# A replanned start: batch 0 partly on GpSimd, a shared interface in the planner, and longer fillers on TensorE

## The chip, the cores and the metric

The kernel runs on one core of one Trainium2 chip. The metric is the device time of an execution in microseconds (us), taken over several runs. A core has five engines that run their own instruction queues: TensorE (PE, matrix products; PEld is its weight load), VectorE (DVE), ScalarE (ACT), GpSimd (POOL) and SyncE (SP, which issues the DMAs here). They wait for each other only through semaphores.

## The reference, cut to what matters

Attention over 4 batches, 8 heads, 576 positions of width 64, in two parts that are added: attention over means of 4 positions (144 x 144 scores per head), and local attention over a band of 3 positions to either side. Its output, 2304 tokens of width 512, goes through a two-layer network with a softplus between.

```python
q_d = q.reshape(B, H, Sd, factor, D).mean(axis=3)      # k_d, v_d alike
out_up = np.repeat(sm_attn(q_d, k_d, v_d), factor, axis=2)
mask = np.abs(pos[:, None] - pos[None, :]) < factor
scores = np.where(mask, scale * np.matmul(q, k.transpose(0, 1, 3, 2)), -1000000000.0)
...
attn = attn / (np.sum(attn, axis=-1, keepdims=True) + 1e-09)
x = (out_up + np.matmul(attn, v)) as [2304, 512]
h = x @ w_in                                            # 512 x 2048
g = np.maximum(h, 0.0) + np.log1p(np.exp(-np.abs(h)))
out = g @ w_out                                         # 2048 x 512
```

## The kernel before, in words

**The work.** Attention is done in 16 units (a batch and a pair of heads; units 0 to 3 are batch 0, `u < NPAIR`, called early). The network works on 5 groups of 512 tokens (the last has 256): layer 1 makes for each of 16 blocks `f` of the inner width a bank `h`, layer 2 adds its product into four banks `acc`. Each operand is split into a high and a low part (`xh`/`xl`, `wi..h`/`wi..l`, `gh`/`gl`), and three products are taken of each pair, so a step of layer 1 or 2 is 12 products of 512 columns.

**One unit of attention.** q and k arrive by DMA. Their sums over 4 positions are made (on TensorE in batch 0, as products with the identity into the bank `sums`, line 331; by a reduction on DVE later, line 344, tiles `qd` and `kd`). ACT scales `qd` into `block`. TensorE makes the scores of the means (`psd`, line 379) and of the band (`psc`, lines 432 and 439). DVE takes maxima (`mxd`, `mx`), ACT the exponentials, DVE sums and reciprocals, and the weights are divided (`sd`: on ACT in batch 0; `sc`: on POOL). They are transposed (`pdt` on TensorE, copied by ACT to `sdT`; `sT` on DVE). The sums of v over 4 positions are `vd` (line 360 on DVE in batch 0, lines 365 and 368 on POOL in batch 1 and on DVE later). TensorE makes `po` (lines 530 and 538), DVE adds both parts into `x` (line 558), ACT and DVE split it into `xh` and `xl` (lines 573 and 578).

**Weights.** A block of `w_in` or `w_out` arrives in 64 bits an element, in one of four buffers that rotate under the tag `stage`. ACT makes a narrow copy `top` (line 631), DVE joins it with the rest (line 636), ACT casts the high part (line 655), and DVE, or POOL for `w_in` from block 4 on, subtracts the low part (line 661). A buffer is free for the DMA of the fourth block after it when that is done.

**Between the layers.** Of a bank `h`, ACT makes the softplus in three passes (lines 702, 705, 706), DVE the last step `t` (line 711), POOL the high part `gh` (line 720), and POOL (first group) or DVE (other groups) the low part `gl` (line 728).

**What sets the order.** All of it is recorded as operations with an engine, a cost, a priority and what they read and write. `Plan.order` runs through a planned time and picks for each free engine the ready operation of lowest priority; the engines then execute their lists in that order. `Plan.warm` puts filler products (`busy`, line 829, a product of 384 columns that nobody reads) into the gaps that TensorE has in the plan ahead of layer 1.

## Time and profile before

| what | us |
|---|---|
| median of 3 runs (516.05 to 516.4) | 516.07 |
| the profiled execution | 515.83 |
| its span, first to last instruction | 513.8 |
| PE busy in it | 499.9 |
| DVE busy | 273.4 |
| ACT busy | 249.8 |
| POOL busy | 121.3 |

The profiled execution's time is 2.03 us above its span. The profile lists for each instruction when it ran, and for an engine that stood idle what ended the wait. Products are pipelined and their ends are modelled, so one of them reads longer (0.39 us) than its distance to the next (0.23 us).

### The profile page before, as it was taken

Reading aid. Unit: us, or ns where it says so; the run is one execution under the profiler, and the core shown is the slowest. Engines: PE = TensorE matmul, PEld = TensorE weight load, DVE = VectorE, ACT = ScalarE, POOL = GpSimd, SP = SyncE. Lnnn points to the kernel's source line nnn. Section 1 sums busy time; section 2 is a strip of 40 time slices with the busy share of each in tenths; the row PEclk is TensorE's granted clock in tenths of the full one; section 3 lists DMA queues with packets and bytes.
Section 4 is the critical chain, followed back from the end, with each engine's and each line's share of the span. In section 5 each row is a group of like instructions: output and inputs, shape, how many; then the busy total and the mean of one; then the engine's idle time right before and its main releaser. Section 6 shows DMA issues by size and latency. Waiting matters only on the chain.

```text
span 513.8 us, 12554 instructions
## 1 busy us (share of the span) xinstructions
PE 499.9 (97%) x5407; PEld 414.2 (81%) x5407; DVE 273.4 (53%) x476; ACT 249.8 (49%) x543; POOL 121.3 (24%) x149
## 2 busy tenths in 40 slices
PE   7999889999899999999999999999999999999997
PEld 6877668888678888887888888888888888889996
DVE  4669976989886564545364746352332222223222
ACT  2468887775765444444354334343343233234442
POOL 2101548775751120102010201120100100101110
PEclk9999999999999999999999999999999999999999
DMA  8914744764622311111112212100020000002001
GB/s 269 340 38 130 245 141 151 245 237 154 200 71 80 136 48 57 48 53 50 55 48 90 96 34 70 33 3 1 0 83 0 1 0 0 1 1 83 1 1 41
DMA packets 15798, 42.86 MB, mean 83 GB/s; under 512 B 1792, under 2 KB 2304, under 8 KB 15744
## 3 DMA queue, kind: packets, MB, share of 16 engines
q1 hardware_dynamic: 15744, 42.07, 25.0%
q8 instruction: 42, 0.69, 0.6%
q14 instruction: 12, 0.10, 0.1%
HBM read 37.35 MB, written 4.72 MB: 82 GB/s over the span
## 4 chain that ended last, share of the span: by engine, by line
PE 80%; DVE 10%; ACT 4%; POOL 3%; issue 2%; POOLq 0%; DVEq 0%
PE acc L747 33%; PE h L682 32%; PE po L538 4%; PE sums L331 3%; DVE wro L636 3%; PE psc L439 2%; PE psd L379 2%; PE po L530 2%; PE pdt L508 1%; DVE wri L636 1%; ACT top L631 1%; PE busy L829 1%; POOL gl L728 1%; DVE t L711 1%; ACT t L705 1%
## 5 line engine op out<-in xcount | busy, mean ns | idle before, releaser
L711 DVE SCALAR_TENSOR_TENSOR t<-h,t 128x512 f32<-128x512 f32 (+1 forms) x80 | 50.8, 636 | 142.4 <-ACT t L706 142.4
L720 POOL TENSOR_SCALAR gh<-t 128x512 fp32r<-128x512 f32 (+1 forms) x80 | 52.2, 653 | 302.8 <-PE acc L747 153.1
L702 ACT ACTIVATE t<-h 128x512 f32<-128x512 f32 (+1 forms) x80 | 44.4, 555 | 153.5 <-PE h L682 134.1
L682 PE MATMUL h<-xh,wi0h 128*128 128x512 f32 (+1 forms) x160 | 61.2, 382 | 1.2 <-ACT wi0h L655 1.2
L747 PE MATMUL acc<-gh,wo0h 128*128 128x512 f32 (+1 forms) x160 | 60.2, 376 | 0.8 <-POOL gh L720 0.8
L728 DVE TENSOR_TENSOR gl<-t,gh 128x512 fp32r<-128x512 f32 (+1 forms) x64 | 39.9, 623 | 39.2 <-POOL gh L720 39.2
L747 PE MATMUL acc<-gl,wo0h 128*128 128x512 f32 (+1 forms) x160 | 59.2, 370 | 1.2 <-POOL gl L728 1.2
L682 PE MATMUL h<-xh,wi0l 128*128 128x512 f32 (+1 forms) x160 | 59.6, 373 | 0.6 <-POOL wi0l L661 0.6
L682 PE MATMUL h<-xh,wi1h 128*128 128x512 f32 (+1 forms) x160 | 60.2, 376 | 0.0
L747 PE MATMUL acc<-gh,wo1h 128*128 128x512 f32 (+1 forms) x160 | 59.6, 372 | 0.0
L682 PE MATMUL h<-xl,wi0h 128*128 128x512 f32 (+1 forms) x160 | 59.6, 372 | 0.0
L682 PE MATMUL h<-xh,wi1l 128*128 128x512 f32 (+1 forms) x160 | 59.5, 372 | 0.0
L682 PE MATMUL h<-xl,wi1h 128*128 128x512 f32 (+1 forms) x160 | 59.4, 371 | 0.0
L747 PE MATMUL acc<-gh,wo0l 128*128 128x512 f32 (+1 forms) x160 | 59.3, 370 | 0.0
L747 PE MATMUL acc<-gl,wo1h 128*128 128x512 f32 (+1 forms) x160 | 59.1, 369 | 0.0
L747 PE MATMUL acc<-gh,wo1l 128*128 128x512 f32 (+1 forms) x160 | 59.0, 369 | 0.0
L706 ACT ACTIVATE t<-t 128x512 f32<-128x512 f32 (+1 forms) x80 | 47.3, 591 | 2.5
L705 ACT ACTIVATE t<-t 128x512 f32<-128x512 f32 (+1 forms) x80 | 47.2, 590 | 2.4
L682 PEld LDWEIGHTS h<-xh,wi0l 128*128 128x128 f32 x160 | 30.2, 189 | 6.9 <-POOL wi0l L661 1.1
L682 PEld LDWEIGHTS h<-xh,wi0h 128*128 128x128 f32 x160 | 30.0, 188 | 7.0 <-ACT wi0h L655 1.6
L747 PEld LDWEIGHTS acc<-gl,wo0h 128*128 128x128 f32 x160 | 30.1, 188 | 6.5 <-POOL gl L728 1.5
L747 PEld LDWEIGHTS acc<-gh,wo0h 128*128 128x128 f32 x160 | 30.0, 188 | 6.2 <-POOL gh L720 1.0
(93 smaller groups left out, 827.0 us busy)
## 6 DMA issues: line engine op xcount, KB each, us to landing
wri<-in_w_in_dram SPq DMA_DIRECT2D x16, 511.8 KB, 4.5
wro<-in_w_out_dram SPq DMA_DIRECT2D x16, 511.8 KB, 4.7
vw<-in_vwin_dram SPq DMA_DIRECT2D x16, 384.0 KB, 4.2
qT<-in_qt_dram SPq DMA_DIRECT2D x16, 292.0 KB, 3.0
kT<-in_kt_dram SPq DMA_DIRECT2D x16, 292.0 KB, 5.7
stage<-in_vrow_dram SPq DMA_DIRECT2D x16, 288.0 KB
out_dram<-osb SPq DMA_DIRECT2D x16, 256.0 KB, 2.2
out_dram<-osb SPq DMA_DIRECT2D x4, 128.0 KB, 1.8
```

The lines of the kernel that those rows point to most:

```text
L331: nc.tensor.matmul(sums.t[:, i * SD : (i + 1) * SD], ident, v[:, :, f], start=(f == 0), stop=(f == FACTOR - 1),)
L379: nc.tensor.matmul(pd3()[:, r, :], qb[:, r * RD : (r + 1) * RD], kd.t, start=True, stop=True)
L538: nc.tensor.matmul(po[h].t[j * D : (j + 1) * D, t * HT : (t + 1) * HT], vw.t[kp, t, :], sT.t[kp, t, :HT], start=True, stop=True,)
L636: lambda: nc.vector.scalar_tensor_tensor(out=e(), in0=e(), scalar=13, in1=top.rearrange("p e w -> p (e w)").bitcast(I32), op0=ALU.logical_ ...
L682: nc.tensor.matmul(h.t[:, :n], w[:, cc, fs], x.t[:, cc, :n], start=(cc == 0 and k == 0), stop=(cc == NCC - 1 and k == 2),)
L702: op("ACT", c, pr, lambda: nc.scalar.activation(out=tv(), in_=hh(), func=AF.Abs), r=[h], w=[tt])
L705: nc.scalar.activation(out=tv(), in_=tv(), func=AF.Exp, scale=-1.0)
L706: nc.scalar.activation(out=tv(), in_=tv(), func=AF.Ln, bias=1.0)
L711: lambda: nc.vector.scalar_tensor_tensor(out=tv(), in0=hh(), scalar=0.0, in1=tv(), op0=ALU.max, op1=ALU.add),
L720: lambda: nc.gpsimd.tensor_scalar(out=gh.t[:, :n], in0=tv(), scalar1=1.0, scalar2=0.0, op0=ALU.mult, op1=ALU.add),
L728: lambda: eng[ge].tensor_tensor(out=gl.t[:, :n], in0=tv(), in1=gh.t[:, :n].bitcast(F32), op=ALU.subtract),
L747: nc.tensor.matmul(acc[g][m].t[:, :n], w[:, f % FB, ms], a.t[:, :n], start=(f == 0 and k == 0), stop=(f == NF - 1 and k == 2),)
```

## The change

Every operation that uses the interface to SBUF which DVE and POOL share is marked `port`, and the planner never lets two of them run at once. In batch 0 the sums of q and k go from TensorE to DVE (the reduction of the later batches), the sums of v, the division of `sd` and the low part `xl` go from DVE and ACT to POOL. In the first group of the network the low parts `gl` go from POOL to DVE, as do those of `w_in` from block 4 on, and the sums of v of batch 1. The small constant ahead of the reciprocals is no longer added by a `tensor_scalar`: it stands in the second column of a prepared pair, and a reduction over the pair adds it. Costs of the planner are changed, block 3 of group 0 no longer takes an `acc` bank, the priority of the `w_out` blocks is one later, and each gap of TensorE ahead of layer 1 that holds at least two fillers gets two more.

```diff
+V_POOL = (0,)
+NORM0 = "POOL"
+O_POS = 4
+NSPLIT = 3
+BLOCK0 = "ACT"
+XL_POOL = (0,)
...
-    FILL = 0.2
+    FILL = 0.165
...
-    DMA_RATE = 0.24
+    DMA_RATE = 0.33
...
+        o.kb, o.block, o.port = kb, block, port or eng == "POOL"
...
+                    if o.port and port > t + 1e-9:
+                        continue
...
+                if o.port:
+                    port = o.end
...
                 n = int((o.start - last) / self.FILL)
+                if n > 1:
+                    n += 2
...
-        if early:
+        if u in ON_PE:
             sums = bank("acc", f"sums{u}")
...
-            if early:
-                nc.vector.tensor_reduce(
-                    out=vd.t, in_=vr.t.rearrange("p c j f d -> p c j d f"), axis=AX.X, op=ALU.add
-                )
-                return
-            e = nc.gpsimd if b < 2 else nc.vector
+            e = nc.gpsimd if b in V_POOL else nc.vector
...
-        def recip(x):
-            nc.vector.tensor_scalar(out=x.t, in0=x.t, scalar1=EPS, scalar2=None, op0=ALU.add)
+        def recip(x, pair):
+            nc.vector.tensor_reduce(out=x.t, in_=pair, axis=AX.X, op=ALU.add)
             nc.vector.reciprocal(out=x.t, in_=x.t)
...
-        op("ACT" if early else "DVE", 0.9 if early else 0.65, sT_ - 1, norm_d, r=[smd], w=[sd])
+        op(ne, {"ACT": 1.25, "DVE": 0.75, "POOL": 1.1}[ne], sT_ - 1, norm_d, r=[smd], w=[sd], port=ne == "DVE")
...
+        xe = "POOL" if b in XL_POOL else "DVE"
...
-        pe = "POOL" if which == "i" and f >= 4 else "DVE"
+        pe = "POOL" if WL_POOL(which, f) else "DVE"
...
-        ge = "POOL" if g < 1 else "DVE"
+        ge = GL_ENG(g)
...
+    for x, y in sums2:
+        nc.gpsimd.memset(x, EPS)
+        nc.gpsimd.memset(y, EPS)
```

`ON_PE` is empty, and `WL_POOL` and `GL_ENG` give DVE everywhere.

**Where TensorE begins.** In the kernel before, TensorE's list starts with the sums of unit 0 (each x4 is four products over one tile), and fillers follow after the scores `psd`:

```order
L331 MATMUL sums_138<-qT_116,ident 128x144 x4
L331 MATMUL sums_138<-kT_118,ident 128x144 x4
L432 LDWEIGHTS identb
L432 MATMUL psc_157<-mask,identb 128x384
L439 MATMUL psc_157<-kT_118,qT_116 32x32 x48
L379 MATMUL psd_213<-kd_211,block 96x144 x3
L829 LDWEIGHTS identb
L829 MATMUL busy<-mask,identb 128x384
```

In the changed kernel TensorE's list starts with the band scores of unit 0, which read the mask:

```order
L474 LDWEIGHTS identb
L474 MATMUL psc_152<-mask,identb 128x384
L481 MATMUL psc_152<-kT_126,qT_124 32x32 x48
L418 MATMUL psd_213<-kd_148,block 96x144 x3
L882 LDWEIGHTS identb
L882 MATMUL busy<-mask,identb 128x384
```

The sums are gone from TensorE, for this unit and the other three, and `psd` now reads a `kd` that DVE makes. Of the fillers there are 27 in all in the kernel before (5 behind this first `psd`) and 64 in the changed one (12 behind this first `psd`), spread over eight gaps.

**DVE's list at its start.** In the kernel before, behind the mask, DVE has the sums of v (`vd`) of unit 0 and then its scores:

```order
L795 CAST mask<-base 128x384
L796 MEMSET mask 64x3
L797 MEMSET mask 64x5
L360 TENSOR_REDUCE vd_155<-stage_120 72x256
L464 TENSOR_REDUCE mx_217<-psc_157 128x12
L469 TENSOR_TENSOR sc_219<-psc_157,mx_217 128x384
```

In the changed kernel the sums of q and k stand around the mask instead:

```order
L381 TENSOR_REDUCE qd_146<-qT_124 128x144
L845 CAST mask<-base 128x384
L381 TENSOR_REDUCE kd_148<-kT_126 128x144
L846 MEMSET mask 64x3
L847 MEMSET mask 64x5
L506 TENSOR_REDUCE mx_217<-psc_152 128x12
L511 TENSOR_TENSOR sc_219<-psc_152,mx_217 128x384
```

The reduction of `vd` has left DVE's list, and the mask, which TensorE's first product reads, is complete only behind the reduction of `kd`.

**POOL's list where layer 2 begins.** In the kernel before, POOL makes in the first group the high and low part of each `t`, and low parts of the weights:

```order
L720 TENSOR_SCALAR gh_0_997<-t_0_926 128x512
L728 TENSOR_TENSOR gl_0_1005<-t_0_926,gh_0_997 128x512
L661 TENSOR_TENSOR wi0l<-wri_877,wi0h 128x4x128
L720 TENSOR_SCALAR gh_1_1039<-t_1_1011 128x512
L728 TENSOR_TENSOR gl_1_1060<-t_1_1011,gh_1_1039 128x512
L661 TENSOR_TENSOR wi0l<-wri_938,wi0h 128x4x128
L487 TENSOR_TENSOR sc_1025<-sc_1025,sm_1069 128x384
```

In the changed kernel POOL has at that place, after the three last `xl` of batch 0:

```order
L770 TENSOR_SCALAR gh_0_1057<-t_0_1002 128x512
L770 TENSOR_SCALAR gh_1_1094<-t_1_1051 128x512
L529 TENSOR_TENSOR sc_970<-sc_970,sm_1097 128x384
L770 TENSOR_SCALAR gh_2_1155<-t_2_1072 128x512
L770 TENSOR_SCALAR gh_3_1186<-t_3_1130 128x512
```

and DVE's list there, with the moved low parts in it:

```order
L778 TENSOR_TENSOR gl_0_1066<-t_0_1002,gh_0_1057 128x512
L761 SCALAR_TENSOR_TENSOR t_1_1051<-h_1_965,t_1_1051 128x512
L711 TENSOR_TENSOR wi0l<-wri_976,wi0h 128x4x128
L686 SCALAR_TENSOR_TENSOR wro_996<-wro_996,top_69 128x512
L686 SCALAR_TENSOR_TENSOR wri_1026<-wri_1026,top_68 128x512
L523 TENSOR_REDUCE smp_64<-sc_970 128x12
L445 TENSOR_REDUCE sm_1097<-smp_64 128x12
L446 RECIPROCAL sm_1097<-sm_1097 128x12
L761 SCALAR_TENSOR_TENSOR t_2_1072<-h_2_1005,t_2_1072 128x512
L778 TENSOR_TENSOR gl_1_1104<-t_1_1051,gh_1_1094 128x512
```

POOL keeps `gh` and the division of `sc`; the 16 `gl` of the first group, 12 low parts of `w_in` and the sums of v of batch 1 (two instructions a unit) are on DVE, in one queue with the weights' joins and `t`.

## Rows read from the trace of the kernel before

**Rows 1.** The page, first part: busy time of each engine, its share of the span, and instructions.

```profile
PE 499.9 (97%) x5407; PEld 414.2 (81%) x5407; DVE 273.4 (53%) x476; ACT 249.8 (49%) x543; POOL 121.3 (24%) x149
```

**Rows 2.** The span in three stages: up to the first product of layer 1, from there to 140 us, and the rest. Busy time of each engine (and instructions), the granted clock of TensorE (1.00 is its higher level), the DMA engines' share.

```profile
0.00:43.39 43.39, 38.49 (x839) 31.11 (x840) 26.63 (x55) 21.58 (x68) 7.01 (x21) 1.00 0.60 194
43.39:140.00 96.61, 91.23 (x1085) 72.98 (x1087) 83.08 (x117) 73.72 (x145) 58.62 (x48) 1.00 0.60 199
140.00:513.80 373.80, 370.18 (x3510) 310.11 (x3496) 163.70 (x306) 154.54 (x331) 55.68 (x81) 1.00 0.13 41
```

**Rows 3.** PE's waits from 40 us to the end: waiting line and what it waited for, us in total, times, the longest. These five are all.

```profile
PE psd L379 <- DVE x L558: 1.6, 1, 1.6
PE h L682 <- ACT wi0h L655: 1.2, 1, 1.2
PE acc L747 <- POOL gl L728: 1.2, 1, 1.2
PE acc L747 <- POOL gh L720: 0.8, 1, 0.8
PE h L682 <- POOL wi0l L661: 0.6, 1, 0.6
```

**Rows 4.** The chain that ended last, in order of time: start, length (us), engine, tile, line, instructions. The four pieces of sums, the longest run of fillers, and the band products of the last unit of batch 0.

```profile
3.73 4.42 PE sums L331 x16
...
11.31 4.10 PE sums L331 x16
...
18.45 4.09 PE sums L331 x16
...
26.11 4.11 PE sums L331 x16
...
37.96 2.87 PE busy L829 x17
...
45.68 1.57 PE po L538 x96
```

**Rows 5.** PE in order of time: start, length, instruction, and in brackets the idle time before it. The first and second product with the mask, the one wait between the units of batch 0, the first product of layer 1, the first part of the last unit's `po`, and the `psd` of batch 1.

```profile
7.97 0.50 PE L432 MATMUL psc<-mask,identb 128*128 128x384 bf16 x1
...
15.23 0.34 PE L432 MATMUL psc<-mask,identb 128*128 128x384 bf16 x1
...
35.13 0.98 PE L379 MATMUL psd<-kd,block 128*96 128x144 f32 x6 [1.15 <-DVE sc L469]
...
43.39 0.48 PE L682 MATMUL h<-xh,wi0h 128*128 128x512 f32 x1
...
44.97 0.71 PE L530 MATMUL po<-sdT,vd 72*64 72x144 f32 x8
...
54.24 0.90 PE L379 MATMUL psd<-kd,block 128*96 128x144 f32 x6
```

**Rows 6.** DVE in order of time: the mask's cast and its last piece, and a reduction of q of batch 1.

```profile
4.57 0.36 DVE L795 CAST mask<-base 128x384 bf16<-128x384 f32 x1 [2.98 <-POOL base L791]
...
5.10 0.06 DVE L797 MEMSET mask<- 64x5 bf16 x1
...
48.33 0.74 DVE L344 TENSOR_REDUCE qd<-qT 128x144 f32<-128x576 f32 x1
```

**Rows 7.** DVE's groups from 43.39 to 140 us, by shape: count, busy us, mean ns of one, idle before.

```profile
L636 DVE SCALAR_TENSOR_TENSOR wro<-wro,top 128x512 int32<-128x512 int32 x14 | 16.6, 1187 | 4.2 <-ACT top L631 3.4 <-issue 0.9
L636 DVE SCALAR_TENSOR_TENSOR wri<-wri,top 128x512 int32<-128x512 int32 x15 | 14.1, 941 | 0.0
L661 DVE TENSOR_TENSOR wo1l<-wro,wo1h 128x512 fp32r<-128x512 f32 x7 | 8.9, 1277 | 2.3 <-ACT wo1h L655 2.2
...
L661 DVE TENSOR_TENSOR wo0l<-wro,wo0h 128x512 fp32r<-128x512 f32 x8 | 7.8, 980 | 1.2 <-ACT wo0h L655 1.2
...
L344 DVE TENSOR_REDUCE qd<-qT 128x144 f32<-128x576 f32 x4 | 2.9, 731 | 0.0
```

**Rows 8.** DVE in order of time, two joins of weights one behind the other.

```profile
123.17 2.57 DVE L636 SCALAR_TENSOR_TENSOR wro<-wro,top 128x512 int32<-128x512 int32 x1
125.67 0.68 DVE L636 SCALAR_TENSOR_TENSOR wri<-wri,top 128x512 int32<-128x512 int32 x1
```

**Rows 9.** POOL in order of time, in the same stretch.

```profile
123.11 0.83 POOL L487 TENSOR_TENSOR sc<-sc,sm 128x384 f32<-128x384 f32 x1
123.91 1.29 POOL L728 TENSOR_TENSOR gl<-t,gh 128x512 fp32r<-128x512 f32 x1
```

**Rows 10.** DVE's groups by shape over the whole span, for the kinds that the change moves to it: count, busy us, mean ns of one, idle before.

```profile
L728 DVE TENSOR_TENSOR gl<-t,gh 128x512 fp32r<-128x512 f32 x48 | 33.1, 689 | 29.0 <-POOL gh L720 29.0
...
L365 DVE TENSOR_TENSOR stage<-stage 72x512 f32<-72x512 f32 x8 | 5.4, 679 | 0.0
...
L368 DVE TENSOR_TENSOR vd<-stage 72x256 f32<-72x256 f32 x8 | 3.6, 455 | 2.2 <-PE po L530 1.4
...
L661 DVE TENSOR_TENSOR wi0l<-wri,wi0h 128x512 fp32r<-128x512 f32 x4 | 2.7, 670 | 0.0
```

**Rows 11.** POOL's groups from 200 to 360 us, by shape: `gh`.

```profile
L720 POOL TENSOR_SCALAR gh<-t 128x512 fp32r<-128x512 f32 x24 | 15.5, 646 | 126.2 <-DVE t L711 54.4 <-PE acc L747 53.0 <-DVE sm L481 13.3
```

More of the change, by code (lines that the diff above doesn't have):

```diff
@@ L49 @@
 LAG = 2
+ON_PE = ()
+TOP_POOL = lambda which, f: False
+V_PE = ()
+WL_POOL = lambda which, f: False
+GL_ENG = lambda g: "DVE"
+V_POOL = (0,)
[3 more added lines that the diff above has]
+BLOCK0 = "ACT"
+KD_POOL = ()
+XL_POOL = (0,)
 B0 = (-40, -32, -24, -16)
@@ L341, in attention, with pool_k @@
             for dst, src, kk in ((qd, q, slice(0, S)), (kd, k, slice(REACH, REACH + S))):
+                if src is k and u in KD_POOL:
+                    ks = buf("ks", [P, 2, SD], 1, f"ks{u}", F32, first)
+                    def pool_k(src=src, kk=kk, ks=ks):
+                        v = src.t[:, kk].rearrange("c (s f) -> c f s", f=FACTOR)
+                        nc.gpsimd.tensor_tensor(out=ks.t, in0=v[:, 0:2], in1=v[:, 2:4], op=ALU.add)
+                        nc.gpsimd.tensor_tensor(
+                            out=kd.t, in0=ks.t[:, 0], in1=ks.t[:, 1], op=ALU.add
+                        )
+                    op("POOL", 1.4, sS - 2, pool_k, r=[k], w=[kd, ks])
+                    continue
                 op(
@@ L471, in attention @@
             ),
-            r=rd + [mx], w=[sc],
+            r=rd + [mx], w=[sc], port=not early,
         )
@@ L663, in weight @@
         after = batch0 if hi else ()
-        op("ACT", 0.62, prio - 1, cast, r=[st], w=[("wh", which, f)], after=after)
+        op("ACT", 0.67, prio - 1, cast, r=[st], w=[("wh", which, f)], after=after)
         op(
-            pe, 1.35 if pe == "POOL" else 0.75, prio - 0.5, rest,
-            r=[st, ("wh", which, f)], w=[("wl", which, f)], after=after,
+            pe, 1.35 if pe == "POOL" else 0.7, prio - 0.5, rest,
+            r=[st, ("wh", which, f)], w=[("wl", which, f)], after=after, port=True,
         )
@@ L685, in mm @@
                     )
-        split = [[cc] for cc in range(NCC)] if f < (2 if g else 4) else [list(range(NCC))]
+        split = [[cc] for cc in range(NCC)] if f < (2 if g else NSPLIT) else [list(range(NCC))]
         for ccs in split:
```

100 lines of the change are left out of this document (60 added, 40 removed).

## The prediction

> **What bounds the kernel now.** I read the busy times first, then the stages, then PE's waits, and last the engines in order of time around the places that the change touches. PE is busy 499.9 of 513.8 us [rows 1], so PE sets the end, and the question is where it does work that can go or stands still. The three stages [rows 2] say where. From 140 us on PE is busy 370.2 of 373.8 us, and the missing part is mostly the tail behind the last product: the change doesn't touch this stage in its work, only in where it begins. From the first product of layer 1 at 43.39 us [rows 5] to 140 us PE is busy 91.2 of 96.6 us: the gap of 5.4 us is the whole of PE's waits, 1.6 + 1.2 + 1.2 + 0.8 + 0.6 [rows 3]. DVE is busy 83.1 us in the same 96.6, so this stage has two engines near their limit. Up to 43.39 us PE is busy 38.5 us, but much of this is not work of the network: four pieces of sums [rows 4] and 27 fillers. So there are two places to win or lose: how early layer 1 can run, and how often PE waits in the 97 us after.
>
> **Part 1: the start, up to the last product of batch 0.** All in PE time, against the same list of other products.
>
> *Sums leave PE.* The four pieces are 4.42 + 4.10 + 4.09 + 4.11 = 16.7 us, one behind the other with the rest on PE [rows 4]. DVE takes 8 reductions of 0.74 us for them [rows 6], 5.9 us, and is busy only 26.6 of the 43.4 us of this stage [rows 2], from which the v sums and `xl` also go to POOL, busy 7.0 us there. So I cost it at -16.7, covered by DVE's idle time.
>
> *PE begins later.* It began at 3.73 us with the sums [rows 4]. Now its first product reads the mask. The mask's cast starts at 4.57 and takes 0.36 [rows 6], to 4.93; then come the reduction of k (0.74) and two small fills, the later of which ended 0.23 us behind the cast in the kernel before [5.10 + 0.06 - 4.93, rows 6]: some 5.9 us, or up to 6.7 if k is there only when PE came to its second half, the sums of k (3.73 + half of 4.42, some 5.9 us; then 0.74 and the fills). That is +2.2 to +3.0; I take +2.5.
>
> *Fillers.* 64 in place of 27, 37 more. Seventeen in a row take 2.87 us, 0.17 each [rows 4]: +6.3. Sixteen of them, 2.7 us, are the "two more than planned". These fillers also cover the time in which DVE, ACT and POOL do their part of the chain, so I add no waits for that; the 1.15 us that PE waited between two units [rows 5] goes, -1.15. If the cover is too short, each of the eight gaps adds a wait, and the nearest row for one is that same 1.15 us: at most +9.2 (rival A).
>
> *The first fillers.* The first product with the mask took 0.50 us, the second, 7 us later, 0.34 [rows 5], though the granted clock is 1.00 over the stage [rows 2]. PE was less used before the first. In the changed kernel the 12 fillers behind the first `psd` come early: 0 to 12 x 0.16 = 1.9 us; I take the middle, +1.0.
>
> The other products (`psc`, `psd`, `pdt`, `po`) are the same and only change place: the last unit's `po` (0.65 + 1.57 us, [rows 4, 5]) and the first `psd` of batch 1 (0.90, [rows 5]) now stand ahead of layer 1 and not behind its first products, which costs nothing in sum. Sum of part 1: -16.7 + 2.5 + 6.3 - 1.15 + 1.0 = **-8.1 us** (ends: -16.7 + 2.2 + 6.3 - 1.15 = -9.4, and with 3.0 and 1.9, -6.7, before any wait in the gaps).
>
> **Part 2: the first group of layer 1.** Here DVE takes work over, and loses waits. It takes, by the uncontended rows [rows 10]: in the stretch to 140 us 13 `gl` x 0.69 = 9.0, 12 low parts of `w_in` x 0.67 = 8.0, four units' v sums x (0.68 + 0.455) = 4.5; together 21.6 us. What it loses: an instruction of DVE that reads two tiles of SBUF reads much longer while POOL works. The clearest case: a join of weights took 2.57 us while POOL ran `sc` and `gl` back to back, and 0.68 the next time, behind the end of `gl` [rows 8, 9]. Against 0.68, the groups of rows 7 are longer by 29 joins: 30.7 - 19.7 = 11.0; 7 + 8 low parts: 16.7 - 10.2 = 6.5; together 17.5 us, while the reduction of q stays at its 0.73 [rows 7]. So DVE's need in this stage goes from 83.1 to 83.1 + 21.6 - 17.5 = 87.2 us if POOL disturbs it no more at all. POOL keeps 13 `gh` of 0.65 [rows 11] and 3 `sc` of 0.83 [rows 9], 10.9 us in which it can still hold DVE up: need 87 to 98 us. I take a third of it, 91. PE's work in this stage is 91.2 less what has moved ahead (2.2 + 0.9), 88.1 us.
>
> That is close, but these two needs are not one chain: PE's work runs at a step of layer 1 with one of layer 2, and DVE may lag behind with weights that are due later. The five waits of before sat at the head of the stage (weights) and at 137 us. Of them the two on POOL's `gl` and `gh`, 2.0 us, had POOL's queue as their cause, which is now short; those on weights (1.8 us) may stay, since DVE now joins and splits all of them and `gl` stands behind joins in DVE's queue [the order of DVE in the section on the change]: a join that waits for its DMA holds `t` and `gl`, and so layer 2. I take 3 us of waits in place of 5.4 (ends: 0, and 98 - 88 = 10). **-2.4 us**, between -5.4 and +4.6.
>
> The Trainium skill ("SBUF — State Buffer", section Who interferes with whom) says that the pair of ports of VectorE and GpSimd is an exclusive lock: whichever instruction starts first holds it to its end, the other is blocked in full; a VectorE instruction with two SBUF inputs contends with a GpSimd one that reads SBUF, a reduction doesn't. The trace agrees [rows 7 to 9]: 2.57 us against 0.68, and 0.73 for the reduction. The rule speaks against the change in one point: `gh` still reads SBUF and all that was moved to DVE has two inputs there. By the rule each `gh` and `sc` that starts first costs DVE its full length, which is rival D below.
>
> **Sum.** -8.1 - 2.4 = -10.5 us. The profiled execution took 515.83 us, its span and 2.03 around it; 515.83 - 10.5 = **505.3 us**. The median of the runs is 0.24 above the profiled one, less than the terms are known to.
>
> **Rivals.**
>
> *B. The waits go altogether.* The planner now knows the shared interface, so its order may fit what runs, and PE waits for nothing after its start: -9.4 to -8.1 and -5.4. 515.83 - 13.5 = 502.3, at best 501. For it: DVE's 17.5 us of prolonged instructions are the cause of late weights. Against it: the head of the stage, where all weights are still to be joined.
>
> *A. The start gives half back.* The fillers stand in for planned gaps; where DVE's queue, which now has eight reductions more, is later than planned, PE waits behind the fillers too. With 5 us of waits in the eight gaps (of 9.2 at most): 505.3 + 5 = 510.3. For it: in-order queues, and POOL now sits in the chain of batch 0 with v sums and `xl`. Against: the two fillers more per gap are 2.7 us of slack.
>
> *D. The interface stays contested.* Each `gh` and `sc` blocks DVE for its full length: need 98 us for 88.1 of PE, 10 us of waits in place of 3: 512.3.
>
> *C. Slower: DVE becomes the engine that sets the first group.* Its mechanism: the moved low parts now stand in DVE's queue, and the prolongation doesn't go but is only met by `gh`, because with DVE full there is always an instruction of it that waits. Need 83.1 + 21.6 = 104.7 and the 10.9 of POOL's rest on top, 115.6 us, against 88.1 of PE: 27.5 us of waits in place of 5.4, +22.1, less 8.1 from the start: 529.8. It decides the sign from the point where the waits exceed 5.4 + 8.1 = 13.5 us, a need of DVE of 101.6 us. For it: DVE at 83.1 of 96.6 us already. Against: POOL's work in the stage falls from 58.6 us [rows 2] to some 11, and the rows show prolonged instructions only beside POOL's.
>
> *E. The change does nothing*: the fillers and the chain in batch 0 eat the 16.7 us. That needs all of the 9.2 us of waits in the gaps, and the old 5.4 later; the time is then some 516.
>
> **How the numbers follow.** Chances: 505.3 as worked out (503 to 508.5) 0.55; B 0.15; A 0.13; D 0.09; C 0.05; E 0.03. The range 500.5 to 512.5 holds nearly all of the first, most of B and A and half of D: 0.8. It is faster by over 0.2% (1 us, about what a measurement of this kernel can tell from no change) in the first, B, A and D: 0.92; within 0.2% in E: 0.03; slower in C: 0.05.
>
> **What would show it.** No `sums` on PE; PE's first product at 5.9 to 6.7 us; the first product of layer 1 at 36 to 38 us with batch 0 already complete (43.39 - 8.1 + 2.2 + 0.9 = 38.4 by the sum). In the start, idle time of PE between the units under 1 us; more means A. Joins and low parts on DVE near 0.7 us on the mean; 0.9 and more means D or C. PE's waits behind the start about 3 us in all, on weights or `gl`, all before 140 us. The rest of the span as long as before. Wrong I would be if PE's clock falls in the start, if a wait on a DMA of weights sits in DVE's queue ahead of `gl` for several us, or if waits appear after 140 us.

## The result, and the profile after

The changed kernel takes 507.34 us (median of 4 runs, 506.1 to 508.24), the one before 516.06 beside it: a ratio of 0.9829 (95% interval 0.9803 to 0.9856). Forecast were 505.3, from 500.5 to 512.5. The profiled execution took 508.24 us, 7.6 less than that of before; its span is 506.3 us, 7.5 less. In what follows "the kernel" without a word is the changed one.

From the page: busy time of each engine (to be held against [rows 1]), the clock granted to TensorE in 40 slices of 12.7 us, and the queue that brings instructions (packets, MB, share).

```profile
PE 494.2 (98%) x5380; PEld 407.4 (80%) x5380; DVE 269.4 (53%) x512; ACT 244.9 (48%) x527; POOL 91.1 (18%) x133
...
PEclk9979999999999999999999999999999999999999
...
q8 instruction: 42, 0.69, 0.6%
```

PE is still the bound, with 5.7 us less work. POOL lost 30 us, DVE grew by no busy time at all. The third digit of the clock, 7, is new; it covers 25 to 38 us.

The three stages, columns as in [rows 2]:

```profile
0.00:43.12 43.12, 35.37 (x922) 27.01 (x922) 27.26 (x64) 20.40 (x59) 22.47 (x40) 0.92 0.59 206
43.12:140.00 96.88, 96.25 (x1084) 77.58 (x1078) 84.20 (x152) 74.57 (x149) 20.63 (x20) 1.00 0.63 202
140.00:506.30 366.30, 362.57 (x3382) 302.84 (x3380) 157.90 (x297) 149.92 (x319) 48.03 (x73) 1.00 0.12 39
```

The first product of layer 1 begins at 43.12 us, nearly where it began before (43.39), but now with batch 0 complete. In the second stage PE is busy 96.25 of 96.88 us (before: 91.23 of 96.61). The third is as full as before and only begins with less left to do. PE's waits from 36 us to the end are one line, where [rows 3] has five:

```profile
PE h L732 <- DVE t L761: 0.5, 1, 0.5
```

DVE's groups beyond 53 us in the stretch to 140, to be held against [rows 7, 10]:

```profile
L778 DVE TENSOR_TENSOR gl<-t,gh 128x512 fp32r<-128x512 f32 x13 | 10.5, 807 | 0.9 <-POOL gh L770 0.9
...
L686 DVE SCALAR_TENSOR_TENSOR wro<-wro,top 128x512 int32<-128x512 int32 x12 | 9.0, 746 | 0.7 <-ACT top L679 0.7
L686 DVE SCALAR_TENSOR_TENSOR wri<-wri,top 128x512 int32<-128x512 int32 x12 | 8.2, 686 | 0.0
```

The joins fell from 1187 and 941 ns to 746 and 686. `gl` reads 807 ns beside POOL's `gh` and 689 without [rows 10]. So DVE took over work that was priced at 21.6 us, and its busy time in the stage rose by 1.1 us, 83.1 to 84.2. POOL now loses time on its side: in that stretch its 15 `gh` take 845 ns on the mean against 646 [rows 11], its four `sc` 1666 ns against 830 [rows 9]. With 20.6 us of work in 96.9 it can afford that, and none of PE's waits is on POOL.

Now the start, PE in order of time (columns as in [rows 5]):

```profile
5.86 0.48 PE L474 MATMUL psc<-mask,identb 128*128 128x384 bf16 x1 [5.86 <-DVE mask L847]
...
9.24 2.36 PE L882 MATMUL busy<-mask,identb 128*128 128x384 bf16 x12
...
25.82 0.65 PE L418 MATMUL psd<-kd,block 128*96 128x144 f32 x4 [0.83 <-ACT xh L617]
...
29.74 1.99 PE L582 MATMUL po<-sT,vw 32*64 32x24 f32 x78 [1.06 <-issue]
...
32.62 3.09 PE L882 MATMUL busy<-mask,identb 128*128 128x384 bf16 x9
```

Nine fillers take 3.09 us at 32.6 us, and twelve took 2.36 at 9.2. The stretches of 2 us show why (columns as in [rows 2]; the clock is the third number from the end):

```profile
28.00:30.00 2.00, 0.94 (x39) 0.68 (x39) 1.55 (x5) 1.46 (x5) 0.76 (x1) 1.00 0.01 4
30.00:32.00 2.00, 2.00 (x76) 1.95 (x70) 0.84 (x4) 0.23 (x1) 0.97 (x2) 0.55 0.04 8
32.00:34.00 2.00, 2.00 (x11) 1.31 (x10) 1.91 (x5) 1.51 (x4) 0.00 (x0) 0.50 0.01 4
34.00:36.00 2.00, 2.00 (x9) 1.04 (x7) 1.29 (x3) 0.00 (x0) 0.00 (x0) 0.50 0.00 0
36.00:38.00 2.00, 2.00 (x66) 1.58 (x64) 0.00 (x0) 1.76 (x4) 0.78 (x1) 0.74 0.77 213
```

From 30 to 37 us the granted clock is half, 1.2 instead of 2.4 GHz (the trace has the change at 30.21 and 37.04 us). And the two waits ahead of it, 0.83 and 1.06 us, both stand in the middle of a run of equal products: four of six `psd`, 78 of 96 `po` were left. A product in the middle of such a run has no new input to wait for. The rows of the stretches that end at these two places, and of the kernel before up to its wait of 1.15 us [rows 5] (this one last), count what PE had executed:

```profile
0.00:24.99 24.99, 19.13 (x475) 14.35 (x476) 16.46 (x42) 11.61 (x37) 15.80 (x34) 1.00 0.93 328
0.00:28.68 28.68, 21.99 (x602) 16.58 (x603) 18.60 (x46) 12.87 (x43) 17.86 (x36) 1.00 0.82 290
```

```profile
0.00:33.97 33.97, 30.22 (x603) 24.87 (x603) 18.60 (x37) 14.92 (x50) 5.09 (x19) 1.00 0.75 244
```

Products and weight loads together: 951, 1205, and 1206 in the kernel before (a record can be missing). The releasers that the profile names don't fit either. Behind a real wait PE starts 0.05 us after the releaser's end: the `h` of the one line above starts at 57.09 us, its `t` ended at 57.04, the first row below. But ahead of the stop at 25.82 us ACT's `xh` had ended at 25.06, and in the kernel before DVE's `sc` at 34.80, 0.33 us before `psd` went on (engines in order of time; the last row is of before):

```profile
56.36 0.68 DVE L761 SCALAR_TENSOR_TENSOR t<-h,t 128x512 f32<-128x512 f32 x1
...
24.45 0.61 ACT L617 CAST xh<-x 128x512 fp32r<-128x512 f32 x1
```

```profile
34.24 0.56 DVE L469 TENSOR_TENSOR sc<-psc,mx 128x384 f32<-128x384 f32 x1
```

So the stops hang on the count of instructions, 254 apart, and not on the product. The page's packets of the instruction queue are 0.69 MB / 42 = 16 KB each. My theory became: at the edge of a block of instructions PE stands still when the next block isn't there, above all where it has used up the last one fast. The first run tests it by moving the products.

### The profile page after: what moved, and what is told of

Read it like the earlier page. It is cut to its first block, busy times and chain, and to the rows that moved or that the text cites. A ratio compares the mean times of both kernels' runs of the same rounds, so it can differ in the third digit from the quotient of the medians.

```text
span 506.3 us, 12487 instructions
## 1 busy us (share of the span) xinstructions
PE 494.2 (98%) x5380; PEld 407.4 (80%) x5380; DVE 269.4 (53%) x512; ACT 244.9 (48%) x527; POOL 91.1 (18%) x133
## 4 chain that ended last, share of the span: by engine, by line
PE 96%; DVE 1%; ACT 1%; DMA 1%; issue 0%
PE acc L797 40%; PE h L732 39%; PE po L582 5%; PE psc L481 3%; PE psd L418 3%; PE busy L882 2%; PE po L574 2%; PE pdt L550 2%; DMA qT<-in_qt_dram 1%; DVE qd L381 0%; ACT top L679 0%; DVE kd L381 0%; DVE wo0l L711 0%; PE psc L474 0%; DVE wri L686 0%
## 5 line engine op out<-in xcount | busy, mean ns | idle before, releaser
L770 POOL TENSOR_SCALAR gh<-t 128x512 fp32r<-128x512 f32 (+1 forms) x80 | 50.2, 628 | 345.4 <-PE acc L797 214.1
L778 DVE TENSOR_TENSOR gl<-t,gh 128x512 fp32r<-128x512 f32 (+1 forms) x80 | 52.4, 655 | 42.5 <-POOL gh L770 42.5
L797 PEld LDWEIGHTS acc<-gh,wo1l 128*128 128x128 f32 x160 | 30.1, 188 | 5.7
L732 PEld LDWEIGHTS h<-xh,wi1l 128*128 128x128 f32 x160 | 30.1, 188 | 5.7
```

What stands on the lines that cost most here:

```text
L732: nc.tensor.matmul(h.t[:, :n], w[:, cc, fs], x.t[:, cc, :n], start=(cc == 0 and k == 0), stop=(cc == NCC - 1 and k == 2),)
L770: lambda: nc.gpsimd.tensor_scalar(out=gh.t[:, :n], in0=tv(), scalar1=1.0, scalar2=0.0, op0=ALU.mult, op1=ALU.add),
L778: lambda: eng[ge].tensor_tensor(out=gl.t[:, :n], in0=tv(), in1=gh.t[:, :n].bitcast(F32), op=ALU.subtract),
L797: nc.tensor.matmul(acc[g][m].t[:, :n], w[:, f % FB, ms], a.t[:, :n], start=(f == 0 and k == 0), stop=(f == NF - 1 and k == 2),)
```

## The experiments

**Run 1: the planned fillers only.** The change's two fillers more per gap are left out; 48 remain of 64. At 951 and 1205 instructions stand other products then.

```diff
                 n = int((o.start - last) / self.FILL)
-                if n > 1:
-                    n += 2
```

> The changed kernel without the two fillers more per gap: 48 fillers in place of 64. Theory S (fillers are slack ahead of work that is ready): 16 x 0.17 us earlier at the most, 504.6 to 507 us. Rival (the fillers hold TensorE's clock and stand for waits that come anyway): the same or up to 3 us slower. For the two stops of TensorE in the changed kernel (0.83 us after 951 instruction records of PE and PEld, in the scores psd of unit 3, and 1.06 us after 1205, behind 18 of the 96 band products po of unit 1): theory F (it has used up its fetched instructions) puts them at the same counts of records, and 12 fillers less ahead of them are 24 records, so the first stop moves into the band scores psc of unit 3 (7 of 96 in), the second to about 30 of 96 po products. Theory W (a wait for another engine) leaves them ahead of the same products.

Measured: 509.11 us (508.13 to 512.9), ratio 0.9886 (0.9837 to 0.9935). PE in order of time, three stops:

```profile
20.93 0.53 PE L572 MATMUL po<-sdT,vd 72*64 72x144 f32 x5 [1.23 <-issue]
...
27.10 0.96 PE L479 MATMUL psc<-kT,qT 64*32 64x32 f32 x89 [1.44 <-issue]
...
30.95 2.01 PE L580 MATMUL po<-sT,vw 32*64 32x24 f32 x66 [1.66 <-issue]
```

and the stretches that end at them:

```profile
0.00:19.70 19.70, 13.84 (x348) 10.15 (x349) 13.21 (x33) 7.78 (x25) 12.61 (x31) 1.00 0.92 278
0.00:25.66 25.66, 18.58 (x475) 13.93 (x475) 16.95 (x43) 11.68 (x37) 16.13 (x35) 1.00 0.94 295
0.00:29.29 29.29, 20.77 (x602) 15.77 (x603) 19.55 (x47) 12.87 (x43) 18.28 (x36) 1.00 0.89 284
```

697, 950 and 1205 instructions: the stops stayed at the counts and moved to the products that stand there now (7 of 96 `psc` done, 30 of 96 `po`). The last one also became longer. From the stop's end at 27.10 us PE used its 254 instructions by 29.29, in 2.19 us, and then stood 1.66; in the changed kernel it used them from 25.82 to 28.68, in 2.86 us, and stood 1.06. A filler is two instructions in 0.17 us, a `po` of the band two in 1.59 / 96 = 0.017: fillers use few instructions, and the 16 fillers that I priced at 2.7 us pay part of it back. Theory W, by which the stops would stand ahead of the same products as before, is out. That 64 fillers beat 48 is not settled by this run alone, since the intervals of the two ratios overlap.

**Run 2: the first group's move undone.** POOL makes `gl`, the low parts of `w_in` from block 4 on and the sums of v of batch 1 again.

```diff
-WL_POOL = lambda which, f: False
-GL_ENG = lambda g: "DVE"
-V_POOL = (0,)
+WL_POOL = lambda which, f: which == "i" and f >= 4
+GL_ENG = lambda g: "POOL" if g < 1 else "DVE"
+V_POOL = (0, 1)
```

> The changed kernel with gl of the first group, the low parts of w_in from block 4 on and the v sums of batch 1 back on GpSimd; start and planner as changed. Theory S (sizes read from the two traces: the start gives 3.0 us, the waits that are gone from the first group 4.6): 511.9 us, and waits of TensorE behind its first layer-1 product of 4 to 6 us again. Rival R (the split of the prediction, 8.1 and 2.4): 509.7 us. Rival Q (the planner's new costs and its rule on the shared interface took the waits away, not the move): within 1 us of the changed kernel, 507.

Measured: 509.47 us (505.74 to 510.72), ratio 0.9859 (0.9816 to 0.9903). PE's waits after its beginning:

```profile
PE psd L418 <- issue: 2.1, 1, 2.1
PE h L732 <- DVE t L761: 1.2, 2, 1.0
PE acc L797 <- issue: 0.6, 1, 0.6
```

The first of them is the stop at 698 instructions. The third, at 81.9 us, comes at 2728, which is 697 + 8 x 254 within 1: a stop too. What is left behind the first product of layer 1 is 1.2 us on `t`, in place of the 5.4 of before, so theory S's 4 to 6 us of waits didn't come. The time lies at rival R's 509.7, but not for R's reason: three of the four runs lost clock (0.993 to 0.997), and the one at 1.0 took 505.74 us, no more than the changed kernel at that clock (506.1 and 506.57). Most of the old waits are gone even with the old division of work between POOL and DVE, which the prediction had no term for.

**Run 3: the start undone.** The sums are on TensorE again, the v sums of batch 0 on DVE in one reduction, `sd` on ACT, `xl` on DVE.

```diff
-ON_PE = ()
+ON_PE = (0, 1, 2, 3)
...
-V_POOL = (0,)
-NORM0 = "POOL"
+V_POOL = ()
+NORM0 = "ACT"
...
-XL_POOL = (0,)
+XL_POOL = ()
...
+            if early:
+                nc.vector.tensor_reduce(
+                    out=vd.t, in_=vr.t.rearrange("p c j f d -> p c j d f"), axis=AX.X, op=ALU.add
+                )
+                return
```

> The changed kernel with batch 0 as before: sums of q and k on TensorE, v sums and xl on VectorE, sd divided on ScalarE; the first group as changed. Theory S: 507.3 + 3.0 = 510.3 us, waits of TensorE in the first group under 1.5 us. Rival R: 515.4 us. Stops by theory F: again after about 951 and 1205 records if those come in a run of short products; the kernel before had its one wait of 1.15 us after 1206 records.

Measured: 510.86 us (510.48 to 511.83), ratio 0.9901 (0.9877 to 0.9925). Of PE's waits behind the first product of layer 1 one is worth a row; 0.2 us more is behind a copy of ACT:

```profile
PE h L737 <- DVE t L766: 1.1, 1, 1.1
```

The step from this kernel to the changed one, the move of batch 0, is 0.9901 - 0.9829 = 0.0072, 3.7 us, where part 1 had 8.1: theory S's 510.3 came within 0.6 us, R's 515.4 did not. The stops that were looked for after 951 and 1205 records stayed away. Two stretches of this run also bear on the clock:

```profile
30.00:32.00 2.00, 2.00 (x99) 1.97 (x96) 1.84 (x4) 1.91 (x9) 0.00 (x0) 0.86 0.03 8
32.00:34.00 2.00, 2.00 (x58) 1.46 (x60) 2.00 (x3) 1.54 (x4) 0.00 (x0) 0.50 0.71 213
```

The clock falls here too, though no wait of PE between its beginning and 34 us is longer than 0.41 us. A stop is not needed for a fall.

**Run 4: the planner without the rule of the shared interface.** Operations marked `port` may be planned at the same time; costs and moves stay. The order that comes out has 55 fillers.

```diff
-                    if o.port and port > t + 1e-9:
-                        continue
```

> The changed kernel, whose planner may again let two operations use the shared interface at once. Theory S (GpSimd has too little left in the first group to collide): within 1.5 us of the changed kernel, joins of weights near 0.75 us. Rival Q (the order by the rule is what keeps the waits away): 2 to 5 us slower, waits of TensorE in the first group above 2 us.

Measured: 508.44 us (505.23 to 512.07), ratio 0.9853 (0.9792 to 0.9915). PE's waits behind the first product of layer 1:

```profile
PE acc L795 <- DVE gl L776: 1.1, 1, 1.1
PE h L730 <- DVE t L759: 0.6, 1, 0.6
```

DVE's joins of `w_out` stay short (14 of 767 ns on the mean, against 746), those of `w_in` grow a little (782 ns against 686): most of POOL's work that made them long is gone either way. Without the rule PE waits 1.7 us there instead of 0.5; in time these runs can tell no difference. The four runs lie at mean granted clocks of 0.997, 0.998, 0.986 and 0.986, and take 506.38, 505.23, 510.5 and 512.07 us: the two low clocks are the two long runs.

**Run 5: four fillers more per gap instead of two.** 80 fillers.

```diff
-                    n += 2
+                    n += 4
```

> The changed kernel with four fillers more than planned in each gap in place of two, 80 in all. Theory K (fillers cost 0.17 us each where TensorE's list is on the path, and buy the higher clock): granted clock nearer to 1.000 over the runs than in the changed kernel (0.992, 0.997, 1.000, 1.000 there), and a base that is up to 2.7 us longer: 506.5 to 509 us. Rival N (the clock falls as before, whatever the fillers): 509 to 511 us, clock 0.99 to 0.997.

Measured: 507.65 us (506.94 to 509.06), ratio 0.9826 (0.9795 to 0.9857): the same as the changed kernel, though 16 fillers are 2.7 us of PE's time. PE's waits over the whole span are these two lines, and the clock is 1.00 over the start:

```profile
PE psc L474 <- DVE mask L847: 5.9, 1, 5.9
PE h L732 <- DVE t L761: 0.9, 2, 0.7
```

```profile
0.00:46.00 46.00, 40.14 (x1050) 30.50 (x1051) 31.13 (x74) 24.72 (x72) 24.84 (x41) 1.00 0.66 211
```

No stop, no fall. The first product of layer 1 begins at 41.20 us, with the same products ahead of it as in the changed kernel and 16 fillers more. 41.20 - 16 x 0.17 = 38.5 us: my sum for this point was 38.4. So the sum of part 1 is right to 0.1 us where neither stops nor the fallen clock come in.

**Run 6: both moves undone.** What stays of the change are the planner's costs and rule, the pairs for the reciprocals and the priorities. 14 fillers come out, 27 stood there before.

```diff
-ON_PE = ()
+ON_PE = (0, 1, 2, 3)
...
-WL_POOL = lambda which, f: False
-GL_ENG = lambda g: "DVE"
-V_POOL = (0,)
-NORM0 = "POOL"
+WL_POOL = lambda which, f: which == "i" and f >= 4
+GL_ENG = lambda g: "POOL" if g < 1 else "DVE"
+V_POOL = (1,)
+NORM0 = "ACT"
...
-XL_POOL = (0,)
+XL_POOL = ()
```

> The changed kernel with both moves undone: batch 0 as before and the first group as before; what is left is the planner's new costs, its rule on the shared interface, the later priority of w_out, block 3 off the acc bank, and the prepared pairs for the small constant. Theory S (the moves are what counts): 515 to 517 us, waits of TensorE in the first group of 4 us and more. Rival Q (the planner's order took the waits away): 510.5 to 513 us, waits under 2.5 us.

Measured: 512.81 us (6 runs, 512.35 to 514.18), ratio 0.9928 (0.9906 to 0.995). This lies below the 515 to 517 that it would take if the two moves were all of the gain. PE's waits from the first product of layer 1 on (all but one of 0.2 us), and DVE's joins in the first group:

```profile
PE acc L802 <- DVE wo1l L716: 1.5, 1, 1.5
PE h L737 <- DVE t L766: 1.1, 1, 1.1
PE pdt L555 <- ACT t L757: 0.8, 1, 0.8
```

```profile
L691 DVE SCALAR_TENSOR_TENSOR wro<-wro,top 128x512 int32<-128x512 int32 x12 | 12.0, 1000 | 3.9 <-ACT top L684 3.9
```

The joins are long again (1000 ns), and yet PE waits only 3.6 us in place of 5.4. With the 13 fillers fewer (2.2 us at 0.17) that accounts for 4.0 us; the ratio says 0.0072 of 516, 3.7 us. So the part of the change that I took for mere bookkeeping is worth about as much as the move of batch 0.

**Run 7: the fillers where the instructions are used fastest.** None more per gap, six ahead of each `po` of batch 0, ordered so that they run before it. 66 fillers.

```diff
-                if n > 1:
-                    n += 2
+                if o.prio < 0 and o.cost == 2.3:
+                    n += 6
...
-                    x.start = last
+                    x.start = last - 1e-6
```

> The changed kernel without the two more per gap, but with six fillers ahead of each po of batch 0: 66 in all, nearly as many as in the changed kernel's 64. Theory F: the first stop, after some 951 records, now falls into psc of unit 3 (1 or 2 of 96 in), the second again at 18 of 96 po products of unit 1, but shorter than 1.06 us by about the six fillers' 1.0 us, because the 254 records between them now last that much longer; less idle time, and the clock falls less often: 505 to 507 us. Rival (only the number of fillers counts, not their place): as the changed kernel, 507 to 508, with stops as long.

Measured: 506.99 us (505.36 to 507.97), ratio 0.9807 (0.9773 to 0.984). One stop is left, inside a run of fillers:

```profile
21.00 0.65 PE L882 MATMUL busy<-mask,identb 128*128 128x384 bf16 x3 [1.21 <-issue]
```

It stands at 697 instructions, not where I expected one; the stops at 951 and 1205, which the theory only wanted shorter, are gone. That is not the fillers' work alone, since PE ran at half clock as it came to 951 and used its instructions more slowly. In time, run 7 and the changed kernel on the same chip (run 8) are not told apart: the intervals overlap. The clock still fell in the profiled execution, from 23 to 30 us, and so did it in one more of the four runs (mean clock 0.992 in both, 1.0 in the others).

**Run 8: the changed kernel once more**, beside runs 5 to 7 on their chip.

> The changed kernel once more, as the measure for the others on the same chip: 506 to 508.5 us; runs with a mean granted clock of 1.000 near 506.3, runs with 0.992 near 508.2, that is about 500 us times the missing share of the clock.

Measured: 507.96 us (507.68 to 510.79), ratio 0.9841 (0.9804 to 0.9878). The two stops are at the same products, with other lengths (the first line shows the fillers at 9.25 us):

```profile
9.25 3.56 PE L882 MATMUL busy<-mask,identb 128*128 128x384 bf16 x12
...
27.10 0.65 PE L418 MATMUL psd<-kd,block 128*96 128x144 f32 x4 [0.83 <-ACT xh L617]
...
30.47 1.35 PE L582 MATMUL po<-sT,vw 32*64 32x24 f32 x78 [0.51 <-issue]
```

The `po` behind the stop takes 1.35 us here and 1.99 in the first profile of the same kernel: with the clock not yet fallen. Place is fixed by the program, length and clock are not. The expectation on the clock held for three of the runs (507.68 to 508.15 us at 0.995 to 0.997); the fourth took 510.79 at 0.992, where 508.2 was expected.

**Run 9: the old costs.** Both moves stay, but the planner works with the costs of before and without the rule. 76 fillers come out.

```diff
-    DMA_RATE = 0.33
+    DMA_RATE = 0.24
...
-                    if o.port and port > t + 1e-9:
-                        continue
...
-            "SP", 0.35, prio - 7,
+            "SP", 0.1, prio - 7,
...
-        op(te, 0.95 if te == "POOL" else 0.75, prio - 2, narrow, r=[st], w=[("top", i)])
+        op(te, 0.95 if te == "POOL" else 0.67, prio - 2, narrow, r=[st], w=[("top", i)])
...
-            "POOL", 0.1 + 0.75 * n / GN, pr,
+            "POOL", 0.1 + 0.54 * n / GN, pr,
```

Some ten more costs go back in the same way.

> The changed kernel with both moves, but the planner's old costs and no rule on the shared interface (two fillers more per gap and the filler's planned length stay as changed; 76 fillers come out of it). The three parts add up so far: planner 4.0 us (before 516.9, both moves undone 512.8), batch 0 3.3, first group 1.9. Theory A (the new costs make the planner's 4 us): 510.5 to 512.5 us, with waits of TensorE in the first group of 3 us and more again. Rival B (the order is no longer critical once the moves are made; the 4 us are of the other small edits): 506.5 to 508.5 us.

Measured: 511.14 us (508.68 to 512.35), ratio 0.9903 (0.9874 to 0.9932), 3.8 us above the changed kernel by the first measurement of that one, 3.2 by run 8's, about as run 6 asks. The small edits that are not costs stayed in, so rival B is out. Three of PE's waits, the first two in the start:

```profile
PE psc L472 <- ACT sd L435: 1.6, 1, 1.6
PE po L580 <- issue: 1.0, 1, 1.0
PE h L730 <- DVE t L759: 0.7, 1, 0.7
```

The 3 us of waits expected behind the first product of layer 1 are not there: they are 1.6 us, 1.1 more than in the changed kernel. The 12 fillers more are another 2 us: the old costs plan longer gaps, and gaps are filled. And the stops are longer, 2.8 us against 1.9; the 1.6 on `sd` is one by its count (950), and `sd` had ended 0.25 us before PE went on. Together 4.0 us. The profiled executions bear this out only with the clock set aside: 508.68 us at 1.0 here, 508.24 in the changed kernel, of which 3.3 us are due to its fallen clock (worked out below), so 3.7; against the changed kernel's two runs at 1.0 it is 2.1 to 2.6. By these lines the new costs pay at least as much in the start as in the first group.

**Run 10: no rule, two more per gap and four ahead of each `po`.** 71 fillers.

```diff
-                    if o.port and port > t + 1e-9:
-                        continue
...
                 if n > 1:
                     n += 2
+                if o.prio < 0 and o.cost == 2.3:
+                    n += 4
...
-                    x.start = last
+                    x.start = last - 1e-6
```

> The changed kernel without the rule on the shared interface, with two more fillers per gap and four ahead of each po of batch 0, 71 in all. Theory K and F together: the stops after 951 and 1205 records get shorter than 0.83 and 0.5 us, the clock falls less than without the rule alone (0.992 on the mean), base near 505: 505 to 506.5 us. Rival: the clock falls as often, 507 to 509.

Measured: 505.95 us (505.88 to 507.71), ratio 0.9803 (0.9778 to 0.9828), the lowest median of all, below both kernels; against the changed kernel, whose interval overlaps with this one, it is not certain. In all four runs the mean granted clock is 0.999 or 1.0. PE's waits after its beginning; the second and third come at 698 and 952 instructions:

```profile
PE acc L797 <- DVE gl L778: 1.2, 1, 1.2
PE psd L418 <- ACT block L396: 0.6, 1, 0.6
PE busy L882 <- issue: 0.5, 1, 0.5
```

So 1.1 us of stops and 1.2 of a wait for `gl` are still in it.

**Run 11: no rule and four more per gap.** 69 fillers, about as many as in run 10, in other places.

```diff
-                    if o.port and port > t + 1e-9:
-                        continue
...
-                    n += 2
+                    n += 4
```

> The changed kernel without the rule on the shared interface and with four more fillers per gap, 69 in all. Theory K: granted clock 0.998 to 1.000 as with four more and the rule, base near 505 to 506: 505 to 507 us. Rival: the clock falls in half the runs, 507 to 510.

Measured: 509.86 us (6 runs, 506.43 to 511.57), ratio 0.9862 (0.9827 to 0.9898). The run of 506.43 us has a mean clock of 1.0, the three of 511.09 to 511.57 have 0.989. Two stretches of the profiled execution:

```profile
28.00:30.00 2.00, 2.00 (x10) 1.63 (x8) 0.00 (x0) 0.00 (x0) 0.23 (x1) 0.57 0.00 0
...
40.00:42.00 2.00, 2.00 (x20) 1.66 (x13) 2.00 (x6) 2.00 (x5) 1.11 (x1) 0.50 0.46 53
```

The clock fell twice. The number of fillers is therefore not what keeps it up.

## Why the prediction was right, and where it was wrong inside

The time came 2.0 us above the forecast, well inside the range, and the nearest rival (A, 510.3) is 3.0 off. But that the total came so near is luck: the sum of -10.5 us, of which 7.6 were measured in the profiled execution, holds two errors of opposite sign. Up to the same set of products (all of batch 0, and what else stands ahead of the first transposition of batch 1) the changed kernel is 2.95 us earlier, where part 1 said 8.1. Behind that PE's waits fell from 5.4 to 0.54 us, 4.85 less, where part 2 said 2.4. (The rest of the span gave 0.2 us back.)

**Part 1, term by term.** *Sums leave PE*, -16.7: it came so, no `sums` stands on PE. *PE begins later*, +2.5: it begins at 5.86 us, +2.1, at the mask's last piece as argued. *First products slow*, +1.0: the size came, in another place; the 12 fillers that it was reckoned for took 2.20 us to the next product, 0.2 more than at 0.17 each, but the first 96 `psc` and the first `psd` ahead of them took 1.05 us more than before. *Fillers*, +6.3: +7.4, since nine of them ran at half clock (1.4 us). *The wait of 1.15 us goes*, and "I add no waits for that": this step failed. The row named DVE's `sc` as what ended that wait, and I believed it; by its count, and by the 0.33 us that `sc` had already been done, it was the stop at 1206 instructions, which ended behind a packet of instructions (last section) and which no shorter chain of engines removes. In the changed kernel two such stops, 0.83 and 1.06 us, stand in its place: +0.75 instead of -1.15. And one term was missing: the clock. The other products of the 7 us at half clock took 1.9 us longer, with the fillers' share 3.3 us. Together -16.7 + 2.1 + 1.05 + 7.4 + 0.75 + 1.9 = -3.5, against the -2.95 that were measured; the other 0.55 us are spread over single products of the start. "If PE's clock falls in the start" stood among the things that would make me wrong, without a price. Run 5, with neither in its start, reaches the forecast's point to 0.1 us once its 16 fillers are taken off.

Two of the signs given for the start failed with it: the first product of layer 1, put at 36 to 38 us, came at 43.12, and PE's idle time between the units was 1.9 us where it was to stay under 1. Two small slips move the sum by no more than 0.2 us: with the two fills the late end of PE's beginning is 6.9 us, not 6.7 (5.94 + 0.74 + 0.23), and the first part of the last unit's `po` is 0.71 us in [rows 5], not 0.65.

**Part 2.** DVE's need was put at 87 to 98 us, and at 91. It was busy 84.2, and the joins came near the 0.7 us asked for; so D and C, which need POOL's rest to hold DVE up for its full length, are out. What is left of the contention: 13 `gl` x 0.12, 12 joins x 0.06, some 3 us with the low parts, of the 10.9 that POOL could take. The step that failed is "I take 3 us of waits in place of 5.4": it was 0.54, and all of it before 140 us, as the prediction had the place. Half of the reason given for the 3 us shows in runs 4 and 10: there `acc` waits 1.1 and 1.2 us for a `gl` that stands in DVE's queue behind two joins, a reduction and two low parts (runs 9 and 11 have such a wait too, 0.6 and 1.1 us). But DVE was busy all through that stretch of runs 4 and 10; no join held it up by waiting for its DMA. In the changed kernel this wait is missing.

**A term that was missing altogether: the planner.** The prediction treated the new costs as what fits the moves, and gave them no number. By the ratios, x 516 us: costs and order alone (run 6) -3.7; the move of batch 0 on top (run 6 to run 2) -3.6, or put in last (run 3 to the changed kernel) -3.7; the move of the first group (run 6 to run 3) -1.4, or put in last (run 2 to the changed kernel) -1.5. Along either path the parts must add up to the whole, 8.8; that both orders give the same parts is what says something. Each is known to some 2 us, so the third alone could also be nothing, and run 2's one execution at clock 1.0 speaks for that. Run 9 finds the planner's share from the other side, 3.2 to 3.8. In it the small edits stayed in (the prepared pairs, the priority, block 3), so the share belongs to the new costs and the rule of the shared interface together. Runs 4 and 10, without the rule, are not clearly slower than the changed kernel, which speaks for the costs; run 4's interval is 6 us wide, and a smaller effect of the rule stays possible. Which of the costs it is was not tried.

**The rivals.** A put the loss of the start into waits in the gaps, 5 us of them. They came to 1.9, and for another reason, the stops; the start lost more by its products at half clock (3.3 us). B, no waits at all behind the start, is nearly what part 2 did (0.54); its time, 502.3, failed by part 1. C and D are refuted by the joins, E by the ratio.

## What to carry to other kernels

When a wait stands in the middle of a run of equal products, or begins again much later than 0.05 us behind the releaser's end, count the instructions up to it, and look where the packets of the instruction queue landed, before believing the releaser. When a planner sets the order, its costs are an edit of their own with a price of their own; run the kernel with them alone. And where runs of one kernel spread, put each time beside its mean granted clock first; it explains much of the spread, though not all.

## What was not expected of the hardware

**Stops at fixed counts of instructions.** From the idle times in PE's order of time (the profile lists those over 0.15 us), and the count of products and weight loads up to each (us; in brackets a count that is off by more than 1; run 10's 0.60 may be in part a wait for `block`):

| kernel | 443 | 697 | 951 | 1205 | 1967 | 2729 |
|---|---|---|---|---|---|---|
| before | | | | 1.15 | | |
| changed, first profile | | | 0.83 | 1.06 | | |
| changed, run 8 | | | 0.83 | 0.51 | 0.36 | |
| run 1 | | 1.23 | 1.44 | 1.66 | | |
| run 2 | | 2.05 | | | | 0.63 |
| run 3 | 0.22 (446) | | | | | |
| run 4 | | 0.22 | 0.83 | 0.51 | | |
| run 5 | | | | | | |
| run 6 | | 0.62 (701) | | | | |
| run 7 | | 1.21 | | | | |
| run 9 | | 0.15 | 1.64 | 0.99 | | |
| run 10 | | 0.60 | 0.54 | | | |
| run 11 | | | 0.76 | | | |

All counts lie 254 or a multiple of it apart. Whether a stop comes at such a count varies, where it can come does not. The Trainium skill ("Runtime: NRT & Kernel Launch", section Instruction fetch mechanics) says that an engine's instructions are refilled in blocks of 16 KiB, 256 of them, ahead of use, and that crossing such an edge is mostly hidden. The trace agrees with the size (packets of 16 KB, steps of 254 in the records) and differs on the cost, which is 0 to 4.3 us a kernel here: hidden in the long products of layer 1, not in the short ones ahead of them.

That a late block is the cause, the packets show. The instruction queue (q8 above) brings 42 of them, and PE's records hold 42 such edges, from 189 on in steps of 254. Every stop in the table ends 1.3 to 1.6 us behind the landing of one packet, and always of the one whose number fits: the second for 697, the third for 951, the fourth for 1205. Eight of the 23 (us):

| kernel | edge | packet begins | lands | PE goes on | behind the landing |
|---|---|---|---|---|---|
| before | 1205 | 32.31 | 33.55 | 35.13 | 1.58 |
| changed, first profile | 951 | 23.31 | 24.33 | 25.82 | 1.49 |
| changed, first profile | 1205 | 26.94 | 28.19 | 29.74 | 1.55 |
| run 1 | 697 | 18.11 | 19.41 | 20.93 | 1.52 |
| run 1 | 951 | 24.55 | 25.58 | 27.10 | 1.52 |
| run 1 | 1205 | 28.14 | 29.35 | 30.95 | 1.60 |
| run 2 | 697 | 19.65 | 20.95 | 22.44 | 1.49 |
| run 8 | 1205 | 28.24 | 29.20 | 30.47 | 1.27 |

At the edges without a stop PE comes at least 1.0 us behind the packet in all thirteen profiles, and mostly by far more. So PE waits for its instructions, and not for another engine. The table also tells why one edge costs more than the next. Where a stop at 1205 follows one at 951, the packet between them begins 1.0 to 1.2 us after PE goes on, and from the end of one stop to the end of the next it is 3.4 to 3.9 us. A stop is what PE's use of 254 records leaves of that time, so fillers between the two edges are nearly paid back there: 2.86 us of use and 1.06 of stop in the changed kernel, 2.19 and 1.66 in run 1 with fewer of them. Ahead of the stops at 443 to 951 the packet begins only 3.4 to 5.5 us after PE crossed the edge before. The DMA engines are 0.93 busy up to 24.99 us and 0.09 from there to 28.68 (changed kernel). That this load makes those packets late fits the numbers; no run changed the load by itself.

**The clock in the start.** In some executions TensorE's granted clock fell to 0.50 for 3.4 to 6.8 us somewhere between 23 and 52 us (in runs 3 and 11 twice), in others of the same kernel not at all. A run's time mostly follows it: the changed kernel took 508.24 us at a mean clock of 0.992, 508.11 at 0.997, 506.57 and 506.1 at 1.0; the kernel before 514.9 at 1.0 and 517.67 at 0.993. It does not always: run 5's longest, 509.06 us, and run 10's, 507.71, were at 1.0. In run 3 it fell with no wait longer than 0.41 us ahead of it, in run 10 two stops of half a microsecond left it at 1.0 in every run, and runs 10 and 11 differ in two fillers and their places while run 11 lost clock in five of six runs. So neither the stops nor the number of fillers decides it alone; what does is open.

The mean leaves something out. The trace's rows of the clock begin at 8.87 us in the kernel before, at 9.73 in the changed kernel's first profile and at 12.18 in run 8, and a view prints 1.00 ahead of them. The products there ran at half pace: in run 8 the fillers stand 0.32 us apart up to 12.1 us, as the nine at a granted clock of 0.50 do in the first profile, and 0.16 behind it; the same 12 fillers took 2.36 us in the first profile and 3.56 in run 8. The 0.50 us against 0.34 from which the prediction took its term for the first fillers [rows 5] is this half pace: the 0.50 stands at 7.97 us, where the 1.00 of [rows 2] is no measurement.
